# A transformer block on one Trainium2 core: the attention's product with v is issued for two units in one run

## The chip, the cores and the metric

The kernel runs on one core of one Trainium2 chip. The metric is the device time of one execution in microseconds (us). A core has TensorE (PE, matrix products into PSUM, with its weight loads listed apart as PEld), VectorE (DVE), ScalarE (ACT), GpSimd (POOL) and SyncE (SP), which here issues the DMAs. PSUM is used as eight banks of 128 x 512 f32.

## The reference

A pre-LayerNorm block over x of shape 1 x 2048 x 448: causal sliding-window attention (16 heads of 28, window 256), then a GEGLU feed-forward part with 1792 hidden columns, each with its residual.

```python
qkv = (x @ wqkv).reshape(B, S, 3, H, Dh)            # H = 16, Dh = 28
scores = einsum("bhqd,bhkd->bhqk", q, k) * Dh ** -0.5
mask = (i - j >= 0) & (i - j < 256)
p = softmax(where(mask, scores, -1e9))
o = einsum("bhqk,bhkd->bhqd", p, v).reshape(B, S, D) @ wo
h  = x + attention(layernorm(x))
h2 = h + (gelu(n @ w_gate) * (n @ w_up)) @ w_down    # n = layernorm(h)
```

## The kernel before

The 16 heads are worked on as four groups of four (g = 0 to 3), the 2048 positions as 16 blocks of 128. A **unit** u = 16 g + t is block t of group g; there are 64. A **chunk** C = 4 g + c is four blocks, 512 positions, of a group; there are 16.

For each unit these steps run. The functions are named as in the listing.

- `scores`: for each of the four heads j, one product of the queries of block t with the keys of up to three blocks (line 541), and on VectorE the masked maximum of each row (line 545).
- `max_split` and `extra`: the negated maxima are split into a high and a low part, transposed on PE (line 570) and copied by ScalarE into rows 96 to 103 of the ring tile (the helper at line 320), so that the next product subtracts them.
- `probs`: for each head one product of the keys of block t with the queries of up to three blocks (line 587), so keys lie on the partitions, and the exponential on ScalarE into tile `pp` (line 591). `pp` has two buffers, chosen by u % 2.
- `select`: GpSimd zeroes the masked corners of `pp`, with one or two operations on all four heads (line 603).
- `attend`: the product of v with `pp` (line 627). Each head's v has 28 columns and a column of ones, so the head's part of the array has 29 columns; the four heads stand at column positions 0, 32, 64 and 96 of the array, all other products use the whole array. A unit adds to the accumulator bank of its chunk and, for t % 4 of 2 or 3, to that of the next chunk as well; two banks (`att`, C % 2) take turns.
- `drain`, after the last unit of a chunk: transpose on VectorE, division by the column of sums, transpose back, split in two parts, and 12 products with the output weights (line 664), added to the residual (line 668).

Ahead of each chunk `project` makes its queries and keys (line 481, 22 products in groups 0 to 2 and 11 in group 3); they go through DRAM and come back shifted into `ring` (`stack`, line 520). In group 3 the second normalisation (`layer_norm`, line 357) runs chunk by chunk, and the first feed-forward products (line 777) fill PE's time. The feed-forward part follows (lines 777 and 806).

The order of the instructions is not that of these loops. Each step is handed to a **planner** (`Lists.op`) with its engine, its cost and latency in us, a key, what it reads and writes, and the PSUM banks that it needs. `Lists.run` then simulates the engines: it repeatedly takes the step that can start first and, among those of an engine that could start within a few hundredths of a us of each other, the one with the lowest key. A step that waits for data, for a bank or for a buffer isn't chosen. The instructions are emitted in that order, each engine executes its own in order, and semaphores hold the data dependences. A key counts scores: those of unit u have 4 u to 4 u + 3. The others lag by constants:

```python
LAG_T = 6    # transposed maxima: 4u + 6
LAG_P = 16   # probabilities: 4u + j + 16; selection: 4u + 20
LAG_V = 22   # product with v: 4u + 22
```

`LAG_V` is also in the keys of `drain`, of the split of the output weights (`wo_weights`) and of the second normalisation. In the planner a product with v is one step of cost 0.214 for each block of 128 queries and 0.33 more. The score banks are 0 and 1, those of the probabilities and the transposed maxima 2 and 3, the accumulators 4 and 5.

Of the kernel before, what the change touches and what calls it, by code (L numbers as in the profile page):

```python
# [8 lines left out]
F32 = mybir.dt.float32  # L9
F32R = mybir.dt.float32r  # L10
BF = mybir.dt.bfloat16
AF = mybir.ActivationFunctionType
OP = mybir.AluOpType
# [3 lines left out]
NT = S // 128  # L17
# [4 lines left out]
SCALE = float(DH) ** -0.5  # L22
RT = 8
RING = (RT + 2) * 128
CS = NT // 4
# [8 lines left out]

LAG_T = 6
LAG_P = 16
LAG_V = 22
EDGE = 11
WIN = 14
FFN = 1000  # L40
# [13 lines left out]
def mm(n):  # L54
    return n / 2400 + 0.0155


def tiles(C):


    return 2 if C < NC - CS else 1

# [13 lines left out]
class Lists:  # L76
# [6 lines left out]
    def op(self, eng, cost, lat, key, fn, r=(), w=(), bank=None, port=False, size=0, tag=None, after=()):  # L83
        o = Op()
        o.eng, o.cost, o.lat, o.key, o.fn, o.port, o.size, o.tag = eng, cost, lat, key, fn, port, size, tag
        o.deps, o.users, o.ready, o.start = set(after), [], 0.0, None
        o.banks = () if bank is None else tuple(bank) if type(bank) is list else (bank,)
        for b in o.banks:
            b.left += 1
        if eng == "pe":  # L90
            w = (*w, *o.banks)
        else:
            r = (*r, *o.banks)
        for toks, wr in ((r, False), (w, True)):
            for tok in toks:
                name, lo, hi = tok if type(tok) is tuple and tok[0] in SPANS else (tok, 0, 1)
                old = self.seen.setdefault(name, [])
                keep = []
                for a in old:
                    if a[0] < hi and lo < a[1] and a[2] is not o:  # L100
                        if wr or a[3]:
                            o.deps.add(a[2])
                        if wr and lo <= a[0] and a[1] <= hi:
                            continue
                    keep.append(a)
                keep.append((lo, hi, o, wr))
                self.seen[name] = keep
        self.ops.append(o)
        if tag is not None:
            self.open[tag] = self.open.get(tag, 0) + 1  # L110
            self.all.setdefault(tag, []).append(o)
        return o
# [96 lines left out]
def block_kernel(ctx: ExitStack, tc, x, wqk_in, wv_in, wo_in, ffn_in, out):  # L209
    nc = tc.nc  # L210
# [3 lines left out]
    op = L.op  # L214

    pool = ctx.enter_context(tc.tile_pool(name="main", bufs=1))
# [25 lines left out]
    rcp = [pool.tile([128, 16], F32, name=f"rcp{i}") for i in range(2)]  # L242
    qk_d = [[dram.tile([GF, 2, 512], F32, name=f"qk{C}_{i}") for i in range(tiles(C))] for C in range(NC)]
    k3_d = [dram.tile([GF, 2, 512], F32, name=f"k3_{c}") for c in range(CS)]
    bank = [psum.tile([128, 512], F32, name=f"bank{i}") for i in range(8)]
# [5 lines left out]
    v012 = vst.enter_context(tc.tile_pool(name="v012", bufs=1, side="right")).tile([128, 3 * VW], F32, name="v012")  # L251
    v3 = fst.enter_context(tc.tile_pool(name="v3", bufs=1)).tile([128, VW], F32, name="v3")
    v012 = v012.rearrange("p (g t h d) -> p g t h d", g=3, t=NT, h=4)
    v3 = v3.rearrange("p (t h d) -> p t h d", t=NT, h=4)
# [3 lines left out]
    late, fa, fp = {}, {}, {}  # L258

    def open_late():  # L260
        lst.close()
        lp = fst.enter_context(tc.tile_pool(name="late", bufs=1))
        for name, shape, dt in (("pp", [128, 2, 4, 384], F32), ("oblk", [128, 512], F32), ("oT", [128, 512], F32),
                                ("wos", [128, 2, D], F32R), ("ohl", [128, 2, 512], F32R)):
            late[name] = lp.tile(shape, dt, name=name)

# [21 lines left out]
    def span(name, lo, n):  # L288
        return (name, lo, lo + n)

    def pp_at(i, j=None):
        return span("pp", 4 * i + (j or 0), 4 if j is None else 1)
# [32 lines left out]
    def dma(key, size, fn, r=(), w=(), cost=0.44):  # L325
        return op("sp", cost, 0, key, fn, r, w, size=size)
# [146 lines left out]

    def project(C):
        g, n = divmod(C, CS)
        for i in range(tiles(C)):
            b = Bank("proj")
# [47 lines left out]
    def rows(toks):  # L525
        return [(*tk, b) for tk in toks for b in range(3)]
# [52 lines left out]
    def probs(u, j):  # L579
        z = min(3, NT - u % NT)  # L580
        k0 = u % RT * 128
        s = 4 * u + j
        b = Bank("prob")
        key = s + LAG_P

        def one():
            nc.tensor.matmul(bank[b.k][:, 0:z * 128], ring[0:104, 1, j, k0:k0 + 128],  # L587
                             ring[0:104, 0, j, k0:k0 + z * 128], start=True, stop=True)

        def exp():  # L590
            nc.scalar.activation(late["pp"][:, u % 2, j, 0:z * 128], bank[b.k][:, 0:z * 128], AF.Exp, scale=SCALE)  # L591
        q = rows([("rk", u % RT)]) + rows([("rq", u % RT + i) for i in range(z)]) + \
            [("rx", u % RT + i) for i in range(z)] + [("pick", i) for i in range(4)]
        op("pe", mm(z * 128), 0.19 + z * 128 / 2400, key, one, q, (), b, tag="prob")
        op("act", 0.065 + z * 0.113, 0.16 + z * 0.113, key, exp, ["late"], [pp_at(u % 2, j)], b, tag="exp")

    def select(u):
        z = min(3, NT - u % NT)
        key = 4 * u + 4 + LAG_P

        def one(o, cm, op_):
            m = late["pp"][:, u % 2, :, o:o + 128]
            nc.gpsimd.affine_select(m, m, pattern=[[0, 4], [-cm, 128]], compare_op=op_, fill=0.0,  # L603
                                    base=0, channel_multiplier=cm)
        op("pool", 0.585, 0.645, key, lambda: one(0, -1, OP.is_ge), [pp_at(u % 2)], [pp_at(u % 2)],
           port=True)
        if z == 3:
            op("pool", 0.585, 0.645, key, lambda: one(256, 1, OP.is_gt), [pp_at(u % 2)],
               [pp_at(u % 2)], port=True)

    acc, early = {}, []

    def attend(u):
        g, t = divmod(u, NT)
        z = min(t + 3, NT)
        parts = []
        for c in range(t // 4, (z - 1) // 4 + 1):
            C = g * CS + c
            if C not in acc:
                acc[C] = Bank(("att", C % 2))  # L620
            parts.append((c, acc[C]))

        def go():
            for c, b in parts:
                lo, hi = max(t, 4 * c), min(z, 4 * c + 4)
                for j in range(4):
                    nc.tensor.matmul(bank[b.k][32 * j:32 * j + DH + 1, (lo - 4 * c) * 128:(hi - 4 * c) * 128],  # L627
                                     (v012[:, g, t, j, :] if g < 3 else v3[:, t, j, :]), late["pp"][:, u % 2, j, (lo - t) * 128:(hi - t) * 128],
                                     start=t == max(4 * c - 2, 0), stop=t == 4 * c + 3, tile_position=(0, 32 * j),
                                     skip_group_check=True)  # L630
        r = [pp_at(u % 2), ("v", t), "ones", "ones3", "cleared"]
        key = 4 * u + LAG_V
        cost = (z - t) * 0.214 + 0.33
        op("pe", cost, cost + 0.2, key, go, r, (), [b for _, b in parts], tag="att")
        if g < 3:
            early.append(L.ops[-1])


    def drain(C):
        g, c = divmod(C, CS)  # L640
        b = acc[C]
        key = 4 * (4 * C + 3) + LAG_V + 1
        last = g == NG - 1
# [27 lines left out]
    def wo_weights(g):  # L671
        key = 64 * g + LAG_V + 12 if g else 18
        dma(64 * g - 20, 224, lambda: nc.sync.dma_start(wo_raw, wo_in[g]), (), [WORAW])
# [147 lines left out]
    for i in range(2):  # L821
        op("dve", 0.4, 0.5, 12 + i, lambda i=i: nc.vector.memset(bank[clear[i].k], 0.0), (), ["cleared"], clear[i],
           tag="clear")
    wo_weights(0)
    for u in range(NU + 2):
        if u < NU:
            if u % 4 == 0:
                project(u // 4)
            if u % 2 == 0:
                stack(u)  # L830
            for j in range(4):
                scores(u, j)
            max_split(u)
            extra(u, Bank("extra"))

        w = u - 2
        if w < 0:
            continue
        for j in range(4):
            probs(w, j)  # L840
        select(w)
        attend(w)
        if w % 4 == 3:
            C = w // 4
            drain(C)
            if C % CS == CS - 1 and C < NC - 1:
                wo_weights(C // CS + 1)
            if C >= NC - CS:
                for t in range(4 * (C % CS), 4 * (C % CS) + 4):
                    layer_norm(t, 4 * (4 * C + 3) + LAG_V + 7 + t % 4, "ln2")  # L850
    op("py", 0, 0, 0, lambda: None, (), ["ringfree"], after=L.all["score"] + L.all["prob"])
# [86 lines left out]
```

## Time and profile before

| | |
|---|---|
| time, median of 3 runs | 786.04 us (784.84 to 786.9) |
| the profiled execution | 783.66 us |
| its span, first to last instruction | 781.9 us |
| mean granted TensorE clock | 0.99 |
| HBM | 45.42 MB read, 18.35 MB written |
| first and last start of a product with v | 82.6 and 360.8 us |

The tables of the profile give, for each engine, busy time and number of instructions. A group's row has line, engine, operation, tiles (out<-in), shape, count, then busy time and mean duration in ns, then the idle time of the engine before them and what ended it. A matmul's duration in the trace is longer than the time by which it holds back the next, since matmuls are pipelined; the distance between starts says more. A product with v in f32 has two records. Times in a stretch count from the start of the span.

### The profile page before, as it was taken

The page shows a single profiled execution, that of the slowest core. Times are in us where ns is not written, and L with a number is a line of the kernel's source. Part 1 is how long each engine was busy: PE and PEld are TensorE (multiplying, and loading weights), DVE is VectorE, ACT ScalarE, POOL GpSimd, SP SyncE. Part 2 cuts the span into 40 slices and gives each one's busy share as a digit, 9 for nine tenths or more (in the row PEclk, how much of TensorE's full clock was granted, in tenths as well). Part 3 has the DMA queues.
Part 4 walks back from the last instruction along what each step waited for, and adds up shares of the span by engine and source line. Part 5 has one row for each costly group of instructions (what it writes and reads, how often), then busy time and mean ns, then how long its engine had stood idle before and what let it go on. Part 6 is the DMA issues. An engine that isn't in the chain of part 4 may idle for free.

```text
span 781.9 us, 11257 instructions
## 1 busy us (share of the span) xinstructions
PE 756.8 (97%) x4022; PEld 604.2 (77%) x4022; DVE 418.4 (54%) x1132; ACT 334.7 (43%) x655; POOL 177.0 (23%) x286
## 2 busy tenths in 40 slices
PE   5999999999999998899999999999999999999997
PEld 5898766777776755566888888888888888888885
DVE  5835887887888778857842243222243322233232
ACT  5564766676677657787621232111131111111111
POOL 8600344343344436666200000000000000000000
PEclk9999999999999989899999999999999999999999
DMA  8434854655675554200320022000000000001111
GB/s 287 142 73 133 244 161 126 187 159 161 177 181 143 167 146 139 85 0 28 129 78 1 0 78 78 0 1 1 0 1 1 0 1 1 1 0 48 48 47 48
DMA packets 43271, 64.50 MB, mean 82 GB/s; under 512 B 5200, under 2 KB 36688, under 8 KB 43216
## 3 DMA queue, kind: packets, MB, share of 16 engines
q1 hardware_dynamic: 43216, 63.79, 27.4%
q8 instruction: 32, 0.52, 0.3%
q14 instruction: 23, 0.19, 0.1%
HBM read 45.42 MB, written 18.35 MB: 82 GB/s over the span
## 4 chain that ended last, share of the span: by engine, by line
PE 88%; ACT 3%; DVE 2%; DMA 2%; SPq 2%; issue 2%; POOL 1%; DVEq 0%; ACTq 0%; POOLq 0%
PE bank L777 35%; PE bank L806 17%; PE bank L481 8%; PE bank L587 5%; PE bank L627 5%; PE bank L664 5%; PE bank L541 5%; PE bank L445 5%; SPq L520 2%; PE bank L357 2%; DMA ring<-qk 1%; PE bank L570 1%; ACT ring L320 1%; DVE mt L545 1%; DMA raw<-in_ffn_dram 1%
## 5 line engine op out<-in xcount | busy, mean ns | idle before, releaser
L591 ACT ACTIVATE pp<-bank 128x384 f32<-128x384 f32 (+2 forms) x256 | 114.7, 470 | 68.3 <-PE bank L587 61.9
L545 DVE CUSTOM_DVE_ANT_0 mt<-bank,mt 128x384 bf16<-128x384 f32 (+2 forms) x256 | 129.7, 525 | 26.2 <-PE bank L541 24.0
L799 DVE TENSOR_TENSOR ge<-bank,ge 128x512 f32<-128x512 f32 x52 | 36.0, 691 | 197.2 <-PE bank L777 196.5
L777 PE MATMUL bank<-xT,ring 128*128 128x512 f32 x528 | 135.8, 391 | 0.0
L777 PEld LDWEIGHTS bank<-xT,ring 128*128 128x128 f32 x528 | 99.0, 188 | 18.2
L603 POOL TENSOR_SCALAR_AFFINE_SELECT pp<-pp 128x512 f32<-128x512 f32 x120 | 74.9, 641 | 134.5 <-ACT pp L591 132.1
L481 PE MATMUL bank<-xT,proj 128*128 128x512 f32 x308 | 104.4, 403 | 0.0
L541 PE MATMUL bank<-ring 84*128 84x384 f32 (+2 forms) x256 | 85.6, 357 | 6.0 <-DVE mx L545 2.8
L797 ACT ACTIVATE ge<-bank 128x512 f32<-128x512 f32 x52 | 31.2, 600 | 139.9 <-PE bank L777 138.4
L777 PE MATMUL bank<-xT,recb 128*128 128x512 f32 x352 | 89.5, 391 | 0.0
L587 PE MATMUL bank<-ring 104*128 104x384 f32 (+2 forms) x256 | 86.5, 354 | 1.8 <-ACT pp L591 0.7
L777 PEld LDWEIGHTS bank<-xT,recb 128*128 128x128 f32 x352 | 66.1, 188 | 12.3
L587 PEld LDWEIGHTS bank<-ring 104*128 104x128 f32 x256 | 48.3, 191 | 23.6 <-ACT pp L591 6.4
L541 PEld LDWEIGHTS bank<-ring 84*128 84x128 f32 x256 | 48.1, 193 | 19.6 <-DVE mx L545 10.5
L481 PEld LDWEIGHTS bank<-xT,proj 128*128 128x128 f32 x308 | 56.7, 190 | 6.5 <-DVE hres L668 0.6
L664 PE MATMUL bank<-wos,ohl 128*128 128x448 f32 x192 | 54.3, 389 | 1.5 <-ACT ohl L320 1.3
L627 PE MATMUL bank<-pp,v 128*29 128x384 f32 (+2 forms) x704 | 53.4, 401 | 0.0
L320 ACT ACTIVATE ring<-bank 8x512 fp32r<-8x512 f32 x80 | 45.2, 583 | 18.1 <-PE bank L570 17.0
L320 ACT ACTIVATE gh<-ge 128x512 fp32r<-128x512 f32 x28 | 17.7, 632 | 81.8 <-DVE ge L799 80.7
L668 DVE TENSOR_TENSOR hres<-bank,hres 128x448 f32<-128x448 f32 x64 | 39.2, 620 | 19.9 <-PE bank L664 19.3
L320 ACT ACTIVATE proj<-ge 128x512 fp32r<-128x512 f32 x28 | 17.7, 632 | 72.8 <-DVE ge L799 72.1
L777 PE MATMUL bank<-xT,reca 128*128 128x512 f32 x176 | 47.4, 395 | 0.0
(97 smaller groups left out, 1080.1 us busy)
## 6 DMA issues: line engine op xcount, KB each, us to landing
ring<-qk SPq DMA_DIRECT2D x210, 112.0 KB
qk<-proj SPq DMA_DIRECT2D x28, 448.0 KB
raws<-in_ffn_dram SPq DMA_DIRECT2D x7, 736.0 KB
raw<-in_ffn_dram SPq DMA_DIRECT2D x7, 736.0 KB
hres<-in_x_dram SPq DMA_DIRECT2D x16, 224.0 KB
out_dram<-hres SPq DMA_DIRECT2D x16, 224.0 KB
ring<-k SPq DMA_DIRECT2D x30, 112.0 KB
raw<-in_wqk_dram SPq DMA_DIRECT2D x7, 256.0 KB
```

The lines of the kernel that those rows point to most:

```text
L320: nc.scalar.activation(dst, src, AF.Copy)
L481: nc.tensor.matmul(bank[b.k], wqk[i][:, h, wb, :], xT[:, xb, n * 512:(n + 1) * 512], start=(a == 0), stop=(a == NP - 1))
L541: nc.tensor.matmul(bank[b.k][:, c:384], ring[0:3 * DH, 0, j, q0:q0 + 128], ring[0:3 * DH, 1, j, kr * 128:kr * 128 + 384 - c], start=True, ...
L545: nc.vector.tensor_tensor_reduce(junk[s % 2][:, c:384], bank[b.k][:, c:384], mask[:, c:384], 1.0, -BIG, OP.add, OP.max, mx[u % 4][:, j:j + 1])
L587: nc.tensor.matmul(bank[b.k][:, 0:z * 128], ring[0:104, 1, j, k0:k0 + 128], ring[0:104, 0, j, k0:k0 + z * 128], start=True, stop=True)
L591: nc.scalar.activation(late["pp"][:, u % 2, j, 0:z * 128], bank[b.k][:, 0:z * 128], AF.Exp, scale=SCALE)
L603: nc.gpsimd.affine_select(m, m, pattern=[[0, 4], [-cm, 128]], compare_op=op_, fill=0.0, base=0, channel_multiplier=cm)
L627: nc.tensor.matmul(bank[b.k][32 * j:32 * j + DH + 1, (lo - 4 * c) * 128:(hi - 4 * c) * 128], (v012[:, g, t, j, :] if g < 3 else v3[:, t, j ...
L664: op("pe", mm(D), 0.38, wk, lambda a=a, oh=oh, wh=wh, i=i, k=k: nc.tensor.matmul(bank[k.k][:, 0:D], late["ohl"][:, oh, i * 128:(i + 1) * 1 ...
L668: op("dve", 0.533, 0.626, wk + 1, lambda t=t, k=k: nc.vector.tensor_tensor(hres[:, t, :], bank[k.k][:, 0:D], hres[:, t, :], op=OP.add), [H ...
L777: op("pe", mm(512), 0.403, kq + a / NP, lambda a=a, h=h, wb=wb, xb=xb, q=q, b=b: nc.tensor.matmul(bank[b.k], get()[q][h][:, wb, :], xT[:, ...
L806: op("pe", mm(D), 0.38, key + 2 * NP + 3 * q + a, lambda a=a, oh=oh, wh=wh, q=q, b=b: nc.tensor.matmul(bank[b.k][:, 0:D], gh(oh)[:, q, :], ...
```

## The change

`attend` takes a pair of units (w - 1, w) with w odd, and issues the products of both as one step of the planner. `pp` gets a third buffer (u % 3), and `LAG_V` goes from 22 to 26, so that the pair has key 4 w + 26. The planner's cost of the step is 0.214 for each block of both units and 0.33 once. The instructions of the products are the same.

```diff
-LAG_V = 22
+LAG_V = 26
...
-        for name, shape, dt in (("pp", [128, 2, 4, 384], F32), ...
+        for name, shape, dt in (("pp", [128, 3, 4, 384], F32), ...
...
-            nc.scalar.activation(late["pp"][:, u % 2, j, 0:z * 128], bank[b.k][:, 0:z * 128], AF.Exp, scale=SCALE)
+            nc.scalar.activation(late["pp"][:, u % 3, j, 0:z * 128], bank[b.k][:, 0:z * 128], AF.Exp, scale=SCALE)
...
-            m = late["pp"][:, u % 2, :, o:o + 128]
+            m = late["pp"][:, u % 3, :, o:o + 128]
...
-    def attend(u):
-        g, t = divmod(u, NT)
-        z = min(t + 3, NT)
-        parts = []
-        for c in range(t // 4, (z - 1) // 4 + 1):
-            C = g * CS + c
-            if C not in acc:
-                acc[C] = Bank(("att", C % 2))
-            parts.append((c, acc[C]))
+    def attend(units):
+        g = units[0] // NT
+        todo, banks, cost = [], {}, 0.33
+        for u in units:
+            t = u % NT
+            z = min(t + 3, NT)
+            cost += (z - t) * 0.214
+            for c in range(t // 4, (z - 1) // 4 + 1):
+                C = g * CS + c
+                if C not in acc:
+                    acc[C] = Bank(("att", C % 2))
+                banks[acc[C]] = True
+                todo.append((u, t, c, acc[C], max(t, 4 * c), min(z, 4 * c + 4)))
 
         def go():
-            for c, b in parts:
-                lo, hi = max(t, 4 * c), min(z, 4 * c + 4)
+            for u, t, c, b, lo, hi in todo:
                 for j in range(4):
                     nc.tensor.matmul(bank[b.k][32 * j:32 * j + DH + 1, (lo - 4 * c) * 128:(hi - 4 * c) * 128],
...
-        r = [pp_at(u % 2), ("v", t), "ones", "ones3", "cleared"]
-        key = 4 * u + LAG_V
-        cost = (z - t) * 0.214 + 0.33
-        op("pe", cost, cost + 0.2, key, go, r, (), [b for _, b in parts], tag="att")
+        r = ["ones", "ones3", "cleared"]
+        for u in units:
+            r += [pp_at(u % 3), ("v", u % NT)]
+        key = 4 * units[-1] + LAG_V
+        op("pe", cost, cost + 0.2, key, go, r, (), list(banks), tag="att")
...
-        attend(w)
+        if w % 2:
+            attend((w - 1, w))
```

More of the change, by code (lines that the diff above doesn't have):

```diff
@@ L262, in open_late @@
         lp = fst.enter_context(tc.tile_pool(name="late", bufs=1))
-        for name, shape, dt in (("pp", [128, 2, 4, 384], F32), ("oblk", [128, 512], F32), ("oT", [128, 512], F32),
+        for name, shape, dt in (("pp", [128, 3, 4, 384], F32), ("oblk", [128, 512], F32), ("oT", [128, 512], F32),
                                 ("wos", [128, 2, D], F32R), ("ohl", [128, 2, 512], F32R)):
@@ L594, in probs @@
         op("pe", mm(z * 128), 0.19 + z * 128 / 2400, key, one, q, (), b, tag="prob")
-        op("act", 0.065 + z * 0.113, 0.16 + z * 0.113, key, exp, ["late"], [pp_at(u % 2, j)], b, tag="exp")
+        op("act", 0.065 + z * 0.113, 0.16 + z * 0.113, key, exp, ["late"], [pp_at(u % 3, j)], b, tag="exp")
     def select(u):
@@ L601, in one @@
         def one(o, cm, op_):
-            m = late["pp"][:, u % 2, :, o:o + 128]
+            m = late["pp"][:, u % 3, :, o:o + 128]
             nc.gpsimd.affine_select(m, m, pattern=[[0, 4], [-cm, 128]], compare_op=op_, fill=0.0,
                                     base=0, channel_multiplier=cm)
-        op("pool", 0.585, 0.645, key, lambda: one(0, -1, OP.is_ge), [pp_at(u % 2)], [pp_at(u % 2)],
+        op("pool", 0.585, 0.645, key, lambda: one(0, -1, OP.is_ge), [pp_at(u % 3)], [pp_at(u % 3)],
@@ L606, in select @@
            port=True)
         if z == 3:
-            op("pool", 0.585, 0.645, key, lambda: one(256, 1, OP.is_gt), [pp_at(u % 2)],
-               [pp_at(u % 2)], port=True)
+            op("pool", 0.585, 0.645, key, lambda: one(256, 1, OP.is_gt), [pp_at(u % 3)],
+               [pp_at(u % 3)], port=True)
     acc, early = {}, []
-    def attend(u):
-        g, t = divmod(u, NT)
-        z = min(t + 3, NT)
-        parts = []
-        for c in range(t // 4, (z - 1) // 4 + 1):
-            C = g * CS + c
-            if C not in acc:
-                acc[C] = Bank(("att", C % 2))
-            parts.append((c, acc[C]))
+    def attend(units):
[11 more added lines that the diff above has]
+                todo.append((u, t, c, acc[C], max(t, 4 * c), min(z, 4 * c + 4)))
@@ L623, in go @@
         def go():
-            for c, b in parts:
-                lo, hi = max(t, 4 * c), min(z, 4 * c + 4)
+            for u, t, c, b, lo, hi in todo:
                 for j in range(4):
                     nc.tensor.matmul(bank[b.k][32 * j:32 * j + DH + 1, (lo - 4 * c) * 128:(hi - 4 * c) * 128],
-                                     (v012[:, g, t, j, :] if g < 3 else v3[:, t, j, :]), late["pp"][:, u % 2, j, (lo - t) * 128:(hi - t) * 128],
+                                     v012[:, g, t, j, :] if g < 3 else v3[:, t, j, :],
+                                     late["pp"][:, u % 3, j, (lo - t) * 128:(hi - t) * 128],
```

## The prediction

> **What bounds the kernel now.** I read the page first. It gives the span and says that TensorE (PE) is busy almost all of it, which by itself does not say where it is the limit.
>
> ```profile
> span 781.9 us, 11257 instructions
> PE 756.8 (97%) x4022; PEld 604.2 (77%) x4022; DVE 418.4 (54%) x1132; ACT 334.7 (43%) x655; POOL 177.0 (23%) x286
> ```
>
> The profiled execution took 783.66 us, its span of 781.9 and 1.8 us around it. The median of the three runs is 786.04, so the profile is 2.4 us quicker than the median. I work out a difference on the profile and take it off the median.
>
> The products of the probabilities with v, line 627, lie between these times (count of records, duration min/median/max in ns, first and last start):
>
> ```profile
> L627 PE MATMUL bank<-pp,v x704: 272/379/847, 82.6 to 360.8; 128*29 128x384 f32 x64, 128*29 128x256 f32 x56, 128*29 128x128 f32 x56
> ```
>
> Next, busy times by stage: attention of head groups 0 to 2, that of group 3, and what follows (columns: window, its length, then busy time with count of PE, weight loads, VectorE, ScalarE and GpSimd, the granted clock, the DMA share, GB/s).
>
> ```profile
> 82.00:274.00 192.00, 189.93 (x1262) 136.61 (x1260) 157.81 (x559) 131.78 (x275) 79.07 (x108) 1.00 0.60 168
> 274.00:362.00 88.00, 81.37 (x490) 52.67 (x491) 66.99 (x211) 62.19 (x129) 52.11 (x87) 0.92 0.29 82
> 362.00:782.00 420.00, 412.79 (x1886) 349.87 (x1884) 147.14 (x235) 97.38 (x162) 10.78 (x16) 1.00 0.08 27
> ```
>
> In the first stage PE is busy for 189.9 of 192 us at full clock, VectorE for 157.8 and ScalarE for 131.8: PE is the bound, VectorE has 34 us to spare and ScalarE 60. In the second PE is busy for 81.4 of 88, at a mean clock of 0.92, with waits. The last stage contains no product with v after the change or before it, and keeps its length.
>
> The waits of the first stage (waiting engine and line, whom it waited for, us in total, times, longest) say the same: PE's own are small, the other engines' waits are for PE.
>
> ```profile
> ACT pp L591 <- PE bank L587: 46.0, 77, 2.2
> DVE mt L545 <- PE bank L541: 16.7, 35, 1.4
> PEld bank L627 <- issue: 10.5, 40, 0.4
> PEld bank L541 <- DVE mx L545: 4.2, 9, 0.8
> ACT pp L591 <- POOL pp L603: 0.9, 1, 0.9
> ```
>
> The row of interest is the third: 40 times in that stage, which has 48 units, the weight load of a product with v stood still although nothing that it needs was missing. The order of time shows what that is (start, length, engine, line):
>
> ```profile
> 84.79 0.52 PE L587 MATMUL bank<-ring 104*128 104x384 f32 x2
> 85.15 0.34 PE L541 MATMUL bank<-ring 84*128 84x384 f32 x1
> 85.42 0.85 PE L627 MATMUL bank<-pp,v 128*29 128x384 f32 x8
> 86.20 0.45 PE L541 MATMUL bank<-ring 84*128 84x384 f32 x1
> 86.48 0.34 PE L587 MATMUL bank<-ring 104*128 104x384 f32 x1
> 86.66 0.27 PE L570 MATMUL bank<-ident,mhl 128*8 128x128 f32 x1
> ...
> 248.48 0.34 PE L541 MATMUL bank<-ring 84*128 84x384 f32 x1
> 248.66 0.34 PE L587 MATMUL bank<-ring 104*128 104x384 f32 x1
> 248.93 0.85 PE L627 MATMUL bank<-pp,v 128*29 128x128 f32 x16
> 249.72 0.27 PE L570 MATMUL bank<-ident,mhl 128*8 128x128 f32 x1
> ...
> 354.97 0.34 PE L587 MATMUL bank<-ring 104*128 104x128 f32 x2
> 355.24 0.64 PE L627 MATMUL bank<-pp,v 128*29 128x256 f32 x8
> 355.80 0.33 PE L587 MATMUL bank<-ring 104*128 104x128 f32 x1
> ...
> 360.67 0.42 PE L627 MATMUL bank<-pp,v 128*29 128x128 f32 x8
> 361.02 0.66 PE L357 MATMUL bank<-ident,xn 128*128 128x128 f32 x4
> ...
> 369.31 0.88 PE L664 MATMUL bank<-wos,ohl 128*128 128x448 f32 x3 [1.26 <-ACT ohl L320]
> ```
>
> **The price of one run.** Ordinary neighbours of 384 columns start 0.18 us apart (248.48 to 248.66, 86.48 to 86.66). Into a run it is 0.27 (85.15 to 85.42, and 248.66 to 248.93), so 0.09 more. A run over three blocks of 128 keys and queries holds PE for 0.78 us (85.42 to 86.20), over two for 0.56 (355.24), over one for 0.35 (360.67): 0.21 for each block and 0.14 that belongs to no block. The matmul that follows a run has the next one 0.28 behind it (86.20 to 86.48), 0.10 more than usual. So entering and leaving costs 0.09 + 0.14 + 0.10 = 0.33 us per run, whatever it computes. And the run of 16 records at 248.93, which writes two banks, takes 0.79 to the next start, no more than one of 8 with the same three blocks: inside a run another group of products pays no entry.
>
> **The change, part by part.** *Two units in a run.* 64 runs become 32. Each pair pays 0.33 us once instead of twice. The products themselves, their loads and the blocks stay the same. In the first stage there are 24 pairs (48 units): 24 x 0.33 = 7.9 us off the engine that sets the end there. The 8 pairs of group 3 save PE 2.6 us, but there PE waits for others:
>
> ```profile
> PEld bank L541 <- DVE mx L545: 6.3, 13, 1.2
> PEld bank L587 <- ACT pp L591: 4.8, 14, 0.8
> PE bank L541 <- DVE mx L545: 2.8, 6, 0.9
> ```
>
> These are of 274 to 362 us alone: 13.9 us of waits of PE for VectorE and ScalarE within 88, more than the 2.6 saved, so what PE saves it waits. I take 0 of it and keep 0 to 2.6 for the range.
>
> *A longer run.* A pair over 3 + 3 blocks holds PE 6 x 0.21 + 0.14 = 1.4 us at a stretch where 0.78 was the most. Queued behind it on PE are the scores (541), whose reader is VectorE, and the probabilities' matmuls (587), whose reader is ScalarE.
>
> ```profile
> L545 DVE CUSTOM_DVE_ANT_0 mt<-bank,mt 128x384 bf16<-128x384 f32 (+2 forms) x184 | 93.2, 524 | 18.2 <-PE bank L541 16.7
> L591 ACT ACTIVATE pp<-bank 128x384 f32<-128x384 f32 (+2 forms) x180 | 81.3, 475 | 48.8 <-PE bank L587 46.0 <-POOL pp L603 0.9
> L545 DVE DVE_READ_ACCUMULATOR2_ANT mx<- 128x1 f32 x184 | 15.2, 83 | 0.0
> ```
>
> Two score banks feed VectorE for 2 x (0.52 + 0.08) = 1.2 us, so it runs dry for 1.4 + 0.34 (the first new score) - 1.2 = 0.5 us in each pair unless other work stands ready. Over 24 pairs that is 13 us against 34 to spare: it fits. PE pays only if it later finds the score banks still full. Now that happens 9 times in 48 units, at 4.2 / 9 = 0.47 us. Bounds: nothing (cover as now) and all 7.9 us of the saving; I take one more such wait at every fifth pair, as often per run as now, 5 x 0.47 = 2.3 us, because the spare time is more than twice the starvation.
>
> *Three buffers and the later key.* The buffers add no instruction. Exponentials of unit w + 2 overwrite unit w - 1, so they now wait for the whole pair (w - 1, w). In the scheduler the pair ranks behind the first two probability matmuls of unit w + 2 (keys 4w + 24 and 4w + 25 against 4w + 26), whose exponentials can't run before it. Behind the waiting exponential ScalarE has queued its copies of the maxima into the ring (320), which later probability matmuls need. I price it at 0, since ScalarE has 60 us of cover, and give the other case to the first rival. Keys of the drain, of the output weights' split and of the second normalisation move by four as well; they stay in their order to one another and to the drain, and add no DMA. The load of those weights (SP) keeps its key.
>
> *The end of attention.* The product of unit 62 (at 355.24) now waits for unit 63 and runs at about 360.7, in front of the last drain: two blocks, 0.4 us, on the path to the output products at 369.31, before which PE even now sits idle for 1.26. Cost 0.4.
>
> **Sum:** -7.9 + 2.3 + 0.4 + 0 = -5.2 us. The profile becomes 778.4, the median 786.04 - 5.2 = 780.8.
>
> **Rivals.** *First, slower: the exponentials wait for the pair.* Per pair of units the first stage takes 192 / 24 = 8.0 us, ScalarE works 131.78 / 24 = 5.5 of these. Between the last exponential of unit w + 1 and the end of the pair it cannot do exponentials.
>
> ```profile
> 247.86 1.67 ACT L591 ACTIVATE pp<-bank 128x384 f32<-128x384 f32 x3 [0.27 <-PE bank L587]
> 249.66 1.22 POOL L603 TENSOR_SCALAR_AFFINE_SELECT pp<-pp 128x512 f32<-128x512 f32 x2 [1.13 <-ACT pp L591]
> ```
>
> The two selections end at 250.88, 1.3 us after the last exponential of their unit (249.53). With the pair taken at once the gap is small, since the next unit's four exponentials, 4 x 0.48 = 1.9 us, run beside the selections. If the key holds the pair back by its four steps of about 1 us each (192 us for 48 units of four), the gap is some 3 us more. It decides from 8.0 - 5.5 = 2.5 us of forced idleness per pair. At 2.7 us all pairs together cost 24 x 0.2 = 5 us: 791. For it: the place of the pair's key, above. Against it: the row with 0.9 us, the only wait of ScalarE for a selection, and the 46 us that it idles for PE now. Chance 0.22.
>
> *Second: the clock.* Group 3 has two dips of the granted clock.
>
> ```profile
> 282.10:285.50 3.40, 2.96 (x12) 1.66 (x10) 3.38 (x14) 3.14 (x7) 1.99 (x3) 1.00 0.41 99
> 285.50:292.30 6.80, 6.80 (x25) 4.14 (x29) 4.18 (x13) 2.65 (x6) 2.69 (x4) 0.50 0.35 104
> 316.20:319.60 3.40, 2.17 (x19) 1.07 (x11) 3.25 (x11) 3.19 (x7) 3.31 (x4) 1.00 0.62 164
> 319.60:326.50 6.90, 6.04 (x31) 4.05 (x31) 6.30 (x27) 2.42 (x4) 2.89 (x6) 0.51 0.30 109
> ```
>
> Each follows 3.4 us with few matmuls, though not idle ones: PE was busy for 2.96 and 2.17 of 3.4. Gathering the products makes the stretches between pairs thinner. A dip of 6.8 us at half the clock costs at most 3.4 us where PE is the limit; one or two more leave -5.2 + 3.4 to -5.2 + 6.8, about 784.2 to 787.6. Chance 0.12. [...]
>
> *Third: no change.* VectorE or the scheduler's order gives all of the 7.9 us back as waits: 786. Against it stand VectorE's 34 us. Chance 0.08. That the cost is paid within a run too, so that nothing is saved, is excluded by the 16 records at 248.93.
>
> *Fourth: all of it.* 32 x 0.33 = 10.6 us, waits of group 3 included: 775.4. Chance 0.10.
>
> **The numbers.** The forecast has 0.48. About 0.3% (2.4 us) is what a measurement of this kernel can tell from no change. Faster: 0.48 + 0.10 + 0.02 of the clock = 0.60. Same: 0.08 + 0.05 of the clock = 0.13. Slower: 0.22 + 0.05 = 0.27. Low end: the fourth rival, 775. High end: 789, which takes in the clock, no change and the nearer part of the first rival. The forecast's own range is 778 to 783.5.
>
> **What would show it.** Right: 32 runs of line 627's successor in place of 64, each of about 1.4 us; the row "PEld L627 <- issue" halved in count; the first stage near 186 us with PE still busy all through; group 3 about as long. Wrong: a new row of ScalarE (exponentials) waiting for the products with v and its 46 us of waits for PE not shrinking; a first stage no shorter while VectorE's waits grow; a third dip in the clock row; a run that takes more than 6 x 0.21 + 0.14.

## The result, and the profile after

The changed kernel takes 781.55 us (median of 5 runs, 778.64 to 784.02), the kernel before 786.04. The ratio is 0.9943, with a 95% interval from 0.9915 to 0.997: faster by about 4.5 us. The forecast was 780.8. A repeat, beside its own runs of the kernel before, gave 0.9933 (0.9903 to 0.9963). The size is right. The experiments show that its parts were not: the later key and the third buffer, which the sum put at 0, give as much without the merging, and the merging adds nothing to them in the time of the whole kernel.

The page after, and the records of the products with v (line 627, now 630):

```profile
span 780.0 us, 11211 instructions
PE 751.5 (96%) x4022; PEld 612.2 (78%) x4022; DVE 417.7 (54%) x1132; ACT 332.5 (43%) x655; POOL 175.7 (23%) x286
L630 PE MATMUL bank<-pp,v x704: 272/379/523, 85.6 to 355.0; 128*29 128x384 f32 x64, 128*29 128x256 f32 x56, 128*29 128x128 f32 x56
```

The work is the same, and the last product with v starts 5.8 us earlier (355.0 against 360.8). But the span is only 1.9 us shorter: the profiled execution took 781.67 us against 783.66. In the order of time a pair that writes two banks looks like this:

```profile
94.34 0.27 PE L570 MATMUL bank<-ident,mhl 128*8 128x128 f32 x1 [0.28 <-ACT pp L591]
94.55 1.50 PE L630 MATMUL bank<-pp,v 128*29 128x256 f32 x32
95.98 0.62 PE L587 MATMUL bank<-ring 104*128 104x384 f32 x2
```

Six blocks in 1.43 us (94.55 to 95.98), 6 x 0.21 + 0.14 + 0.03. Of the 32 runs, 28 are of six blocks and have the next matmul right behind them; all of these take 1.42 to 1.44 us. The price of a run is as forecast, and a pair pays it once. Now the stages, with the windows of the prediction:

```profile
82.00:274.00 192.00, 186.46 (x1279) 142.34 (x1279) 159.96 (x572) 131.86 (x279) 81.19 (x112) 0.99 0.62 174
274.00:362.00 88.00, 80.15 (x477) 55.23 (x477) 66.07 (x198) 63.77 (x129) 52.67 (x86) 0.88 0.24 69
```

The first window now reaches further into the work (1279 matmul records for 1262), but PE is busy for 3.5 us less of it: part of what was saved became idle time. In the second the mean granted clock is 0.88 in place of 0.92.

Windows of time do not hold the same work in two kernels. So I also added up the matmuls of each trace in order, each at the spacing that ordinary neighbours show (0.18 us for 384 columns, 0.23 for 512, 0.21 for a block of the product with v), leaving out switches and products whose result is unused. I then compared the times at which two kernels have done the same sum. The difference is the **lead** (in us; positive is ahead). Against the kernel before, at its 250 and 400 us:

| one trace each | lead at 250 us (groups 0 to 2 nearly done) | lead at 400 us (attention over) |
|---|---|---|
| changed kernel | 3.6 | 2.0 |
| changed kernel, repeat | 4.2 | 3.2 |

By then 20 pairs have been issued, worth 20 x 0.33 = 6.6 us. In these two traces some 55 to 65% of it has arrived, and group 3 then gives a part back. So the lead of the changed kernel does arise in groups 0 to 2, where the sum put it; what the sum had not foreseen is how group 3 depends on the order, and that is what the experiments show.

### The profile page after: what moved, and what is told of

Read it like the earlier page. It is cut to its first block, busy times and chain, and to the rows that moved or that the text cites. A ratio compares the mean times of both kernels' runs of the same rounds, so it can differ in the third digit from the quotient of the medians.

```text
span 780.0 us, 11211 instructions
## 1 busy us (share of the span) xinstructions
PE 751.5 (96%) x4022; PEld 612.2 (78%) x4022; DVE 417.7 (54%) x1132; ACT 332.5 (43%) x655; POOL 175.7 (23%) x286
## 4 chain that ended last, share of the span: by engine, by line
PE 88%; DVE 3%; ACT 3%; SPq 2%; DMA 2%; issue 1%; POOL 1%; DVEq 0%; ACTq 0%; POOLq 0%
PE bank L782 35%; PE bank L811 17%; PE bank L481 8%; PE bank L541 6%; PE bank L587 6%; PE bank L669 5%; PE bank L630 5%; PE bank L445 5%; SPq L520 2%; PE bank L357 2%; DMA ring<-qk 1%; PE bank L570 1%; DVE mt L545 1%; PE bank L890 1%; ACT ring L320 1%
## 5 line engine op out<-in xcount | busy, mean ns | idle before, releaser
L591 ACT ACTIVATE pp<-bank 128x384 f32<-128x384 f32 (+2 forms) x256 | 112.6, 469 | 63.0 <-PE bank L587 56.2
L481 PE MATMUL bank<-xT,proj 128*128 128x512 f32 x308 | 103.1, 402 | 0.0
L782 PE MATMUL bank<-xT,proj 128*128 128x512 f32 x176 | 46.3, 394 | 0.1
```

The lines of the kernel that those rows point to most:

```text
L481: nc.tensor.matmul(bank[b.k], wqk[i][:, h, wb, :], xT[:, xb, n * 512:(n + 1) * 512], start=(a == 0), stop=(a == NP - 1))
L591: nc.scalar.activation(late["pp"][:, u % 3, j, 0:z * 128], bank[b.k][:, 0:z * 128], AF.Exp, scale=SCALE)
L782: op("pe", mm(512), 0.403, kq + a / NP, lambda a=a, h=h, wb=wb, xb=xb, q=q, b=b: nc.tensor.matmul(bank[b.k], get()[q][h][:, wb, :], xT[:, ...
```

## The experiments

All medians are device times; each ratio is to the kernel before, run beside it on the same chip (its median was 785.46 to 786.3 us there, but 788.69 beside e12, so compare e12 by its ratio). The mean granted clock is that of the same runs; for the kernel before it was 0.988 to 0.989. "Fill" is explained below.

| kernel | units per run | buffers | key | fill | median us | ratio (95%) | clock | lead at 250, 400 |
|---|---|---|---|---|---|---|---|---|
| changed | 2 | 3 | 26 | | 781.55 | 0.9943 (0.9915 to 0.997) | 0.9856 | 3.6, 2.0 |
| e11 (repeat) | 2 | 3 | 26 | | 781.67 | 0.9933 (0.9903 to 0.9963) | 0.9870 | 4.2, 3.2 |
| e1 | 2 | 3 | 22 | | 791.34 | 1.007 (1.0048 to 1.0092) | 0.9816 | 0.4, -8.3 |
| e3 | 2, switched | 3 | 26 | | 787.55 | 1.0015 (0.9993 to 1.0037) | 0.9882 | -1.6, -1.1 |
| e7 | 1 | 3 | 22 | | 784.85 | 0.999 (0.9969 to 1.0011) | 0.9902 | 0.2, -0.3 |
| e8 | 1 | 2 | 26 | | 785.2 | 0.9987 (0.9959 to 1.0014) | 0.9899 | -0.7, 0.7 |
| e2 | 1 | 3 | 26 | | 779.79 | 0.9896 (0.9857 to 0.9935) | 0.9913 | -0.4, 3.9 |
| e5 | 1 | 2 | 22 | yes | 780.88 | 0.9938 (0.9915 to 0.996) | 0.9989 | -0.2, 3.6 |
| e4 | 2 | 3 | 26 | yes | 779.63 | 0.9907 (0.9877 to 0.9936) | 0.9970 | 1.9, 3.4 |
| e9 | 1 | 3 | 26 | yes | 775.28 | 0.9854 (0.9827 to 0.988) | 0.9994 | 0.9, 8.0 |
| e6 | 2, then 1 | 3 | 26 | | 780.72 | 0.9942 (0.9913 to 0.9971) | 0.9913 | 1.7, -1.5 |
| e12 | 2, then 1 | 3 | 26 | yes | 777.37 | 0.9874 (0.9839 to 0.991) | 0.9957 | 1.8, 5.2 |
| e10 | 2 | 3 | 24 (LAG_P 14) | | 782.98 | 0.9954 (0.9929 to 0.9979) | 0.9857 | -0.8, -0.6 |

A lead is of one trace and moves by some 2 us between traces of the same order: the five traces with pairs of key 26 up to there lead by 3.6, 4.2, 1.9, 1.7 and 1.8 at 250 us. Three traces have a dip of the clock of 3.4 us near 80 us, which costs them at most 1.7 us from there on: e2, e12 and e10; e10 has another at 121 us. And the trace of e6 is of an execution of 784.95 us, 4 us slower than its median, so its leads are low. I build on medians, and use leads to say where.

**Switches put back (e3).**

```diff
             for n, (u, t, c, b, lo, hi) in enumerate(todo):
+                if n and u != todo[n - 1][0] and g < 3:
+                    nc.tensor.matmul(bank[0][:, 511:512], ident, ident[:, 0:1], start=True, stop=True)
```

> The changed kernel, its order untouched, with one product of the whole array, one column wide, into an unused column of a score bank between the two units of each pair of groups 0 to 2 (24 of them). It puts the leaving and entering back and nothing else. Theory A: 24 x 0.33 = 7.9 us more than the changed kernel, about 788 to 790, above the kernel before. Theory B (the gain lies in order and buffers, the switches are hidden): 781 to 783.

The order of time of this kernel (line 630 is the inserted product, 632 the product with v):

```profile
94.62 0.85 PE L632 MATMUL bank<-pp,v 128*29 128x256 f32 x16
95.40 0.38 PE L630 MATMUL bank<-ident 128*128 128x1 f32 x2
95.72 0.85 PE L632 MATMUL bank<-pp,v 128*29 128x128 f32 x16
96.50 0.62 PE L587 MATMUL bank<-ring 104*128 104x384 f32 x2
```

The same pair now holds PE for 1.88 us (94.62 to 96.50) in place of 1.43, so 0.45 us are put in, a little more than the 0.33 of a run, since the inserted product has a weight load and two records of its own. 24 x 0.45 = 10.8 us of PE time cost 6.0 us of time (787.55 against 781.55; 5.7 to 6.4 by the ratios), between the two theories. So the switches are on the path, but only some 55% of their time reaches the end. That is near the lead of the changed kernel, 3.6 and 4.2 of 6.6. Two things blur the share. The inserted product writes into a score bank, and six maxima of VectorE waited for it, 5.0 us in all, so the edit adds a little more than a switch. And the mean clock of e3 is higher than the changed kernel's (0.9882 against 0.9856 and 0.9870), which hides a part of its cost.

**The key and the buffers apart from the merging (e2, e7, e8, e1).** Each is a change of constants; e2, for example, is the kernel before with

```diff
-LAG_V = 22
+LAG_V = 26
-("pp", [128, 2, 4, 384], F32)
+("pp", [128, 3, 4, 384], F32)        # and u % 3 for u % 2
```

e7 has only the buffers, e8 only the key, and e1 is the changed kernel with `LAG_V = 22`.

> The kernel before with three buffers and LAG_V 26, units still issued one by one (64 runs). Theory A (runs merged): no gain, 785 to 787. Theory B (buffers and key bring it): 781 to 783.

> The kernel before with three buffers alone: single units, LAG_V 22. Theory G (a third buffer lets the exponentials run on): 779 to 782. Theory H (only with the later key is anything gained, as the product with v no longer goes first): 785 to 787.

> The kernel before with LAG_V 26 alone: single units, two buffers. Theory G or H alike: the exponentials of unit u + 2 then wait for the product of u, so no gain or a loss, 786 to 795. If the key alone brings the gain of single units with both: 779 to 782.

> The changed kernel with LAG_V back at 22: pairs and three buffers as they are, only the place of the pair in the planner's order changes. Theory A (the gain is the 0.33 us that each merged run no longer pays, and the key is only a place in the order): within 1.5 us of the changed kernel, 780 to 783. Theory B (the later key is needed, or brings the gain, since a pair taken as soon as it is ready takes PE from scores and probabilities): 784 to 787, with more waits of VectorE and ScalarE for PE.

Theory A, on which the prediction stood, has fallen in two of these. Single units with both constants, which save no switch (their traces still have 64 runs), are faster by 5.7 us (779.79 against 785.46), as much as the changed kernel or more. And pairs without the later key are slower than the kernel before, 791.34, more than either theory expected. Beside e7, which has the same buffers and key and single units (784.85), the pairs cost 6.5 us there. Neither constant does it alone (784.85 and 785.2, both intervals contain 1). The waits of ScalarE between 82 and 345 us say why the key needs the buffer. First the kernel before, then the key alone, then the key with three buffers and single units, then the changed kernel:

```profile
ACT pp L591 <- PE bank L587: 58.9, 97, 2.2
```

```profile
ACT pp L591 <- PE bank L587: 38.6, 86, 2.1
ACT pp L591 <- PE bank L627: 16.3, 10, 3.0
```

```profile
ACT pp L591 <- PE bank L587: 50.8, 90, 1.6
```

```profile
ACT pp L591 <- PE bank L587: 51.7, 77, 2.0
ACT pp L591 <- PE bank L630: 3.1, 4, 1.8
```

With two buffers the later key makes the exponentials wait 16.3 us for the product with v, which frees their buffer, and so most of what they no longer wait for the probability matmuls is lost again (38.6 + 16.3 against 58.9). That is the mechanism of the first rival. The third buffer takes this row away for single units and leaves 3.1 us of it for pairs. What the later key then gains is seen in group 3 (274 to 362 us) of e2:

```profile
274.00:362.00 88.00, 82.76 (x495) 54.75 (x495) 72.46 (x214) 66.79 (x134) 55.89 (x88) 0.92 0.31 87
```

VectorE is busy for 72.5 us of this window where it was for 67.0, and ScalarE for 66.8 instead of 62.2. In the kernel before a product with v goes almost as soon as its data are there; with the later key more of the scores and probabilities, which feed the two engines that PE waits for here, go ahead of it. The last probability product starts at 346.2 us in e2, at 356.9 in the kernel before. The lead grows from -0.4 at 250 us to 3.9 at 400. That the order of these products is the cause is my reading of these rows; no run changes it in group 3 alone.

**Without the dips of the clock (e4, e5, e9).** In these the planner's filler, which at the start of the kernel transposes a constant into a free bank when PE would be idle, is allowed in group 3 as well. The results are not used.

```diff
-        if t > WARM or t + cost > until or ...
+        if (t > WARM and not 262.0 < t < 345.0) or t + cost > until or ...
```

> The changed kernel, with small transposes of a constant into free banks where the planner sees PE idle in group 3 (119 of them, results unused), so that the clock has no thin stretch to fall in. Theory C (the dips of the clock in group 3, 24 us at half in the profile of the changed kernel against 13.7 before, gave part of the gain back): no dip or one, 774 to 778. Rival D (VectorE and ScalarE set the pace there, so a slow PE costs nothing): 780 to 783 whatever the clock does.

> The kernel before with the same fill in group 3 (99 transposes, results unused). With the filled changed kernel at 779.6 it gives the change without the dips of the clock. Theory C (dips gave part of the gain back): the kernel before gains less from the fill than the changed one, 784 to 786, and filled against filled the change is worth 5 us or more. Rival (the dips fall on both alike, or cost nothing): 782 or less, and filled against filled under 4 us.

> Single units with three buffers and LAG_V 26, and the fill of group 3: the filled changed kernel (779.6) without its merging, both without dips. Theory I (merging saves its switches but pays them back in waits for ring loads and in dips; without dips it keeps a part): 780 to 782, one or two us above the filled changed kernel. Theory J (merging brings nothing at all here; buffers and key are the whole gain): 776 to 779.

The changed kernel's own dips, each behind the window before it:

```profile
265.40:268.80 3.40, 2.17 (x11) 1.50 (x10) 2.28 (x10) 2.28 (x6) 1.25 (x3) 1.00 0.65 136
268.80:272.20 3.40, 3.40 (x11) 2.62 (x11) 2.80 (x11) 3.19 (x8) 2.40 (x3) 0.51 0.72 192
299.60:303.00 3.40, 2.03 (x7) 1.00 (x6) 2.39 (x9) 3.35 (x7) 3.39 (x3) 1.00 0.33 97
303.00:309.80 6.80, 6.59 (x18) 5.23 (x18) 5.25 (x18) 4.93 (x11) 4.89 (x7) 0.50 0.57 167
313.20:316.60 3.40, 1.19 (x8) 0.69 (x6) 3.33 (x9) 2.06 (x4) 3.31 (x4) 1.00 0.26 83
316.60:323.40 6.80, 6.80 (x22) 4.84 (x22) 4.91 (x18) 5.42 (x10) 5.32 (x13) 0.50 0.61 172
```

With a fourth at 282.5 us that is 24 us at half clock inside attention, against 13.7 before (the trace of the repeat has three dips, 17 us): the second rival, in part. The clock of all runs says the same, 0.9856 and 0.9870 against 0.989. Among the runs of the kernel before (four sets, of 11 to 34 runs) a mean clock lower by 0.001 goes with 0.56 to 0.74 us. By this slope, an estimate, the lower clock of the changed kernel is worth 1 to 2.5 us. It is at most that: with the fill its clock rises by 0.010 or more, some 6 us by the slope, and 2 to 3 us arrive by the ratios.

With the fill the clock stays up in the traces, as the list of cores says for e4, e5 and e9:

```profile
core 0: 778.7 us, clock 0.999
core 0: 778.5 us, clock 1.000
core 0: 773.5 us, clock 1.000
```

The filled changed kernel (779.63) lies between Theory C and Rival D. Theory C expected the kernel before to gain less from the fill than the changed one. It gained more (0.9938), and filled against filled the change is worth 1.2 us by the medians and 2.4 by the ratios, which is not clear of no change. So dips took from the change, but are not what decides. The sharpest comparison is e9 with e4: the same buffers, key and fill, and only the merging differs (with it goes that the first unit of a pair waits for the second). Single units take 775.28, pairs 779.63; the two intervals of the ratio meet only at their edges (0.988 and 0.9877). In the two traces, which have no dip inside attention, it is 775.28 against 780.43. The pairs take about 4 us more, although merging saves PE up to 32 x 0.33 = 10.6; a part, some 1.5 us by the slope above, may be clock, since the other runs of e4 have lost a little (0.9970 on average). Theory J was right. The windows of group 3, e9 ahead of e4:

```profile
274.00:362.00 88.00, 85.83 (x582) 62.10 (x581) 74.93 (x220) 68.77 (x137) 56.60 (x90) 1.00 0.33 96
274.00:362.00 88.00, 83.21 (x618) 63.60 (x611) 67.40 (x208) 65.54 (x133) 54.81 (x87) 1.00 0.25 72
```

With single units VectorE is busy for 74.9 us of the window, with pairs for 67.4, at full clock in both. (The counts of matmuls include the fill.) The loss lies in group 3: the pairs lead by 1.9 at 250 us against 0.9, and by 3.4 at 400 against 8.0. In group 3 of e4 a product with v starts on average 4.5 us after the last selection of its unit, in e9 0.9 us.

At key 22 the pairs cost 6.5 us, at key 26 about 4 or less. No run gives them a key later than 26, so these runs do not show the best that pairs can do.

**Pairs in groups 0 to 2 only (e6, e12).**

```diff
-        if w % 2:
+        if w >= 48:
+            attend((w,))
+        elif w % 2:
             attend((w - 1, w))
```

> The changed kernel with pairs in groups 0 to 2 only and single units in group 3; three buffers and key 26 everywhere. Theory E (merging pays where PE is the bound, up to 260 us, and costs in group 3, where buffers and key gain 4 us by themselves): 775 to 778, under both the changed kernel and single units with three buffers. Rival F (group 3 falls out by chance of the order, so gains do not add): 780 to 785. At equal work the stage of groups 0 to 2 is ahead of the kernel before by 4 us at 260 in both theories.

> Pairs in groups 0 to 2, single units in group 3, three buffers, LAG_V 26, and the fill of group 3. Theory M (merging is worth 2 to 4 us in groups 0 to 2 and costs about 5 in group 3, and the two add): 771 to 774, under the filled single units (775.3). Rival F (what group 3 takes depends on the state in which the planner's order enters it, not on merging there): 776 to 781.

If the merging paid in groups 0 to 2 and cost in group 3, and the two were independent, these would be the fastest of all. They are not: 780.72 and 777.37, both in the range of Rival F, with ratios near those of the changed kernel and between e4 and e9. So Theory E, and M after it, did not hold, though e12 cannot be told from e9 by its ratio. The lead of about 4 us that both theories expected of e6 ahead of group 3 is not in its trace either (1.7). Why group 3 seems to take longer behind pairs, even where it has none itself, is not settled: from 250 to 400 us e12 gains 3.4 and e9 7.1, and a dip of 3.4 us in e12 explains at most 1.7 of this. Late products with v do not explain it, as those of group 3 start 0.7 us after the selection in e12. The planner's whole order there differs between these kernels, and no run isolates one wait.

**Earlier probabilities (e10).** The loads into the ring must wait for the last probability matmuls that read the old rows (line 587). The waits of SP and of PE in groups 0 to 2 (82 to 256 us), before and then after:

```profile
SPq L520 <- PE bank L541: 20.2, 10, 6.8
SPq L520 <- PE bank L587: 1.4, 2, 1.2
PE bank L541 <- DMA ring<-qk: 1.6, 2, 1.0
PEld bank L541 <- DVE mx L545: 3.9, 8, 0.8
DVE mt L545 <- PE bank L541: 15.2, 33, 1.4
```

```profile
SPq L520 <- PE bank L541: 27.9, 10, 4.8
SPq L520 <- PE bank L587: 7.0, 5, 4.0
PE bank L541 <- DMA ring<-qk: 3.0, 2, 1.6
PEld bank L541 <- issue: 2.2, 2, 2.0
PEld bank L541 <- DVE mx L545: 4.3, 8, 1.7
PEld bank L587 <- issue: 3.3, 7, 0.6
PEld bank L587 <- ACT ring L320: 2.0, 5, 0.6
DVE mt L545 <- PE bank L541: 9.5, 17, 2.4
```

The waits of the scores for the ring's loads have grown from 1.6 to 3.0 us; the row of 2.2 us that ends by "issue" may belong to them, but the profile does not say so. Those for VectorE have hardly grown. (In the trace of the repeat the row for the loads is 1.4 us, so the growth is not in every trace.) So I brought the probabilities forward:

```diff
-LAG_P = 16
-LAG_V = 26
+LAG_P = 14
+LAG_V = 24
```

> The changed kernel with the probabilities two keys earlier (LAG_P 14, LAG_V 24). Loads into the ring are issued some 0.4 us after the last probabilities that read the old contents, so this should bring them forward by up to 2 us. Theory K (PE now waits for ring loads, 5 to 9 us in groups 0 to 2 against 2 before): these waits under 3 us, 777 to 780. Rival L (the copies of the maxima come too late then): waits for the ring copies of ScalarE grow by as much, 781 to 785.

```profile
PE bank L541 <- DMA ring<-qk: 1.9, 1, 1.9
PEld bank L587 <- issue: 7.1, 14, 0.6
PEld bank L587 <- ACT ring L320: 0.2, 1, 0.2
```

The wait for the ring fell to 1.9 us as Theory K expected, but the time did not: 782.98, at the clock of the changed kernel (0.9857). That its trace has no lead at 250 us says little, since two dips of the clock, at 80 and 121 us, lie ahead and cost it up to 3.4 us. Making this wait smaller gained nothing; another grew in its place (from 3.3 to 7.1 us before probability matmuls). The rival's growing wait for the copies of the maxima did not come either (from 2.0 to 0.2 us). The longest wait of SP for the ring, that for the scores which read the old rows (20.2 us before, 27.9 after), was not the aim of any run.

The repeat (e11):

> The changed kernel again, beside the next two on one chip. Both theories: 780 to 783, a mean clock under that of the kernel before. If it comes out under 779, its distance to single units with both constants was chance.

It came out as expected. The fastest version is e9, which has no merging: 775.28 us, 0.9854 of the kernel before, against 0.9933 for the changed kernel on that chip.

## Why the prediction was right in size and wrong in its parts

- *The price of a run, 0.33 us.* Right: a pair holds PE for 1.43 us, and putting switches back costs time. The 32 runs and their length came as named.
- *24 x 0.33 = 7.9 us "off the engine that sets the end there".* Right in place, too large in size. PE was busy for 99% of the stage, but of 6.6 us 1.7 to 4.2 arrived at 250 us in five traces, and of 10.8 us put back 6.0 reached the end. What PE is spared turns in part into idle time: in the first window it idles 5.5 us where it idled 2.1.
- *2.3 us for the longer run, as waits for VectorE with full score banks.* Misnamed, and somewhat too small. That row stayed (3.9 us before, 4.3 after, 3.5 in the repeat); 2.4 to 4.9 us of 6.6 were lost, in waits spread over several releasers. The cover named, VectorE's spare time, was there: its own waits for scores fell from 15.2 to 9.5 us.
- *Buffers and key at 0.* This step failed most. Alone each is 0; together, with single units, they are worth 5.7 us. I priced the later key only as a danger and didn't ask what the products with v, taken first, had been holding up in group 3, where VectorE and ScalarE are waited for. For pairs the key matters even more: 791.34 with 22, 781.55 with 26.
- *Group 3 at 0 for the pairs.* Wrong in sign: the changed kernel loses 1.0 to 1.6 us of its lead there (3.6 to 2.0, and 4.2 to 3.2 in the repeat), a part of it by dips. The gain that buffers and key bring with single units (-0.4 to 3.9) does not appear with pairs, and about 4 us lie between pairs and single units with the fill. The rule "PE waits there, so what it saves it waits" left out that the order in group 3 can cost or gain time by itself. By which wait it does so stays open.
- *The end of attention, 0.4 us.* No run separates it.
- *The first rival* (exponentials wait for the pair): its mechanism is real, 16.3 us with two buffers, and the third buffer leaves 3.1. *The second* (the clock): came true in part, with 24 us of dips for 13.7 in one trace and 17 in the repeat, worth 1 to 2.5 us at most. *The third and fourth* did not come.
- *The signs named.* The row "PEld L630 <- issue" did not halve: it was 13.5 us in 52 times before and is 14.0 in 58, since weight loads now stand still inside the longer runs too, where PE is not idle. So it is no count of the switches. A third dip of the clock, a sign of being wrong, did come.

So the number is in good part luck. The sum had a saving by merging of 7.9 - 2.3 us and nothing for the constants. Measured one after the other, the constants with single units give 5.7 us, and merging on top of them gives none. These two errors cancelled. The steps do not simply add: merging before the key is moved costs 6.5 us, and moving it then gives some 10 back.

## What to carry to other kernels

A change of three parts is three predictions. Price the constants beside the main edit as carefully as the edit, and run each alone, because here the main edit was the part without gain of its own. An engine at 99% need not pass on all that it is spared: here it was some half, and putting a known cost back is a test of that. In an order planned ahead, a lower priority for a long step can be worth more than making it cheaper, if there is a buffer for what it holds.

## What the runs showed of the hardware

The granted clock fell to half after windows in which PE was far from idle: 2.17 us of records in 3.4 us, and 2.96 in the kernel before. The dips inside attention lasted 3.4, 6.8 or 10.2 us. In e4, e5 and e9, 119, 99 and 75 short transposes of a constant in the gaps kept it up: mean clock 0.997 to 0.999 in place of 0.986 to 0.991, and 4.8 us for the kernel before (0.9938). With 57 of them, in e12, one dip in group 3 was left. No run shows from which activity on the clock stays up. And the mean clock goes with much of the scatter between runs of one kernel: among 34 runs of the kernel before, from 781.38 to 790.08 us, it lay between 0.984 and 0.996, with a correlation of -0.84.
